# Key-value sums and quotients in two 64-column halves instead of four 32-column quarters, with a rewritten step list

## The chip, the cores and the metric

The kernel runs on one core of one Trainium2 chip. The metric is device time in microseconds of one execution; three executions of the kernel before gave 562.0 to 562.4 us, median 562.02 us. The trace that is read below is a fourth, profiled execution.

## What is computed

The input is q, k and v of 4 batches x 8 heads x 576 positions x 64. Attention with 128 random features comes first, then two layers of experts with one expert per token; the second layer reads what the first gives. In float32, cut to what matters here:

```python
q_p, k_p = phi(q_s), phi(k_s)                  # phi: project on omega (128 x 64), subtract a max, exp
kv = np.einsum('bhsm,bhsd->bhmd', k_p, v)      # sums of keys and values: 128 x 64 per head
z = np.sum(k_p, axis=2)
num = np.einsum('bhsm,bhmd->bhsd', q_p, kv)
den = np.einsum('bhsm,bhm->bhs', q_p, z)[..., None] + 1e-06
attn = num / den                               # the quotients
# x: 2304 tokens x 512; each of two layers, for each token's best of 8 experts e:
h = np.maximum(x[mask] @ w1[e], 0.0)           # 512 -> 1024
out[mask] = gate_w[mask, None] * (h @ w2[e])   # 1024 -> 512 (layer 1 has a second gate as well)
```

## The kernel before

**Attention.** Heads go in 16 pairs (0 to f). For a pair, TensorE projects keys (`k_proj`, L185) and queries (`q_proj`, L219) into tiles `ph`; VectorE takes maxima of the key features (L195), ScalarE makes their exponentials (L199); query features are copied out of PSUM by ScalarE or VectorE, GpSimd takes their maximum over partitions (L226), VectorE subtracts it (L230), ScalarE makes the exponential (L234). Then `kv` (L242) sums keys times values into `pkv`, a copy makes it `kvr`, `num` (L268) multiplies query features by it into `pn`, VectorE divides (L286 to L290), TensorE transposes (L304, `pf`), and copies give the raw activations.

**The two functions that change.** `kv` and `num` have a 128-partition output of 65 columns for each chunk of 128 positions and each head. They cut it into four matmuls, each with 32 columns of the stationary operand, that write to partitions 0, 32, 64 and 96. Each of these float32 matmuls is two matmuls and two weight loads in the trace: 640 in the program of each of `kv` and `num` are 1280 rows each.

**Experts.** Eight units (layer, batch) run in the order `ORDER`. A unit takes the expert that most of its batch chose, splits the expert's weights into a high and a low part (`high` L133 or L131, `low` L488), and multiplies in three terms (`group`, L92, `pm`): 384 matmuls of 288 columns in 64 steps of six. ScalarE and VectorE take each of the first 32 steps' results (`hh` L515, `hl` L516); VectorE multiplies each result of the last 32 by the gate (L534, `y`). `pm` has two PSUM buffers.

**The stray block.** Tokens that did not choose their batch's expert are handled in blocks of up to eight. The one block that these inputs need in layer two is done by `ahead` (flow `A`: choose it, load its data, find its tokens, gather them with GpSimd at L662, multiply by w1, L692 `pu`, transpose, L701 `phf`, multiply by w2, L713 `pyc`, transpose, L721 `pby`, scatter with GpSimd at L732 into `by`). It is then added to an earlier batch's output by `early` (flow `B`: load `old`, add at L753, store at L755) or to the last unit's own rows by `merge` (L548, steps `M7..`) before their store (L557, steps `S7..`). All of it is issued with factors that are zero where it does not apply, so both additions always run.

**What sets the order.** All engines' instructions are issued in the order of the string `PLAN`: a name is one step of attention (first letter the function, then the pair, then the part), of a unit (`F` fetch, `H` high, `L` low, `W` gate row, `X`, `Y` next layer's split, `S` store, `M` merge), of a flow (`G0` to `G7` gate of a unit, `A`, `B`); a `+` means VectorE in place of ScalarE; a number is so many steps of six matmuls of the running unit; `z5` is five idle matmuls on zeros (L836). Each engine runs its own instructions in this order, and waits on semaphores.

Of the kernel before, what the change touches and what calls it, by code (L numbers as in the profile page):

```python
# [48 lines left out]
r100 t01 m01 e010 e011 z5 q11 k10 k11 s00 m11 r110 v00 v01 x00 s01 w0 r111+ t10 m10 e111 e110 x01 z6 q20 k20 r200 s10
r201+ n00 n01 e100 m20 d00 e101 t11 s11 x10 d01 v10 v11 e200 k21 m21 e201 w1 x11 z5 f00 f01 q21 e210 g00 r211 e211  # L50
r210+ g01+ n10 n11 v20 v21 d10 t20 q30 q31 r301 s20 x20 r300+ r311 r310 h0 w2 o0 t21 d11 a5 a6 k30 m30 s21 t31 f10 g10
t30 l0 f11 k31 m31 e301 e300 g11 x21 q40 s31 r400 r401 q41 r410 r411+ a7 e310 h1 o1 e311 n20 n21 s30 d20 x31 d21 t40
l1 k40 k41 b6 x30 v30 v31 w3 f20 g20 m40 f21 s40 e400 m41 e401 g21 t41 s41 n30 n31 e411 e410 x40 d30 d31 h2 k50 k51
m51 x41 v40 v41 e510 f30 l2 e511 w4+ g30 m50 c6 f31 q50 r500 e500 r501+ n40 n41 q51 a8 r510 r511 d40 e501 d41 g31+ o2
b7 t50 t51 z6 k60 k61 h3 l3 m60 o3 m61 G0 v50 v51 G0 e601 e610 c7 s50 G0 G0 s51 f40 f41 g40 g41 G0 G0 x50 e600 w5 e611
o4 z3 k70 m70 x51 G0 P0 F00 F01 k71 m71 v60 v61 n50 e701 d50 e710 e700 c8 G0 w6 e711 n51 d51 q60 q61 H00 r610 a9 r600
r601+ v70 v71 f50 c9 f51 L00 G0 G0 w7+ H01+ t60 g50 g51 F02 1 L01 G0 1 o5 s60 1 F03 2 x60 2 H02+ W0 1 L02 2 H03 1 F04
1 L03 3 F05 1 H04+ 2 L04 2 H05+ 1 F06 1 L05 3 F07 1 H06+ 2 L06 9 H07 L07 2 r611+ t61 2 h4+ l4 h5+ 1 s61 b8 b9 1 l5 1
x61 1 n60 n61 q70 q71 r700 r710+ r711 d60 d61 r701+ aa 1 t70 2 f60 s70 t71 f61 k80 k81 x70 m80 m81 S010 ba g60+ g61+ 1
e801 e800 s71 1 e811 e810 1 h6+ o6 1 v80 v81 w8+ x71 n70 n71 q80 q81 ab r801 r811+ r810 d70 d71 r800+ l6 1 t81 2 f70  # L60
s81 f71 k90 ka0 m90 g70 g71 k91 e900 e901 bb m91 h7 x81 ma0 o7 t80 s80 1 G1 G1 l7 ea01 e910 1 G1 G1 x80 S020 1 G1 G1 1
G1 1 P1 F10 F11 2 G1 2 G1 G1 e911 ka1 G1 bc G2 v90 v91 H10 L10 G2 ma1 S030 w9 n80 n81 d80 d81 G2 W1 F12 G2 H11 1 ea11
ea10 1 L11 2 f80 g80 G2 G2 3 P2 G2 ea00 1 H12 1 G2 1 L12 2 G2 G2 F13 1 F14 G2 1 H13+ 2 L13 2 H14 1 F15 1 L14 3 F16 1
H15 2 L15 2 H16+ 1 F17 1 L16 2 f81 q90 q91 r910 r911+ g81 r901+ F20 r900+ ac S000 X00 Y00 1 t91 o8 h8+ H17+ 1 t90 1 l8
1 s91 L17 3 s90 1 H20 x91 X01+ Y01 1 X02+ F21 1 x90 L20 1 S100 1 Y02 X03+ ca cb 2 F22 1 Y03 1 H21 1 va0 va1 n90 n91 cc
wa qa0 qa1 ra00+ ra10 ra01 ad ra11+ L21 S110 d90 d91 1 ta0 ta1 1 F23 1 sa0 2 f90 f91 kb0 kb1 sa1 bd xa1 mb0 mb1 g90+
g91+ xa0 1 eb01 eb00 1 eb11 eb10 H22+ 1 h9+ na0 na1 vb0 vb1 da0 cd qb0 qb1 rb01+ rb10+ rb00 l9 rb11+ wb+ da1 ae L22 o9
S120 1 tb0 1 tb1 2 sb0 fa0 F24 ga0 2 sb1 xb0 1 xb1 H23 1 nb0 G3 nb1 db0 S130 L23 W2 qc0 qc1 F25 rc10 af rc01+ rc11
rc00 db1 G3 1 fb0 fb1 kc0 kc1 be mc1 gb0+ gb1 mc0 tc1 tc0 1 ec10 sc1 ec11 1 G3 G3 ob 1 ec01 ec00 sc0 1 xc1 1 G3 xc0 G3
1 H24 1 G3 P3 1 L24 3 F26 3 H25+ fa1 kd0 kd1 ga1+ md0 L25 bf md1 vc0 vc1 G4 oa ha+ F27 wc nc0 ed01 nc1 G4 G4 ed10 ce  # L70
dc0 dc1 la hb+ 2 fc0 gc0 1 lb 5 H26 2 L26 3 F30 3 X10 H27 Y10 3 L27 1 F31 4 H30 X11+ Y11 1 X12+ S200 1 L30 1 Y12 X13
Y13 2 F32 G3 ed00 3 H31+ G3 G3 G4 1 G3 L31 S210 1 G4 G4 2 G4 F33 1 P4 2 G4 1 H32 1 G4 L32 G4 1 S220 G4 1 F34 5 H33 1
S230 W3 1 L33 3 F35 3 H34+ 2 L34 3 F36 3 H35+ 2 L35 3 F37 3 H36+ 2 L36 3 F40 3 H37 2 L37 2 F41 4 H40+ 1 S300 1 L40 2
F42 4 H41 1 S310 1 L41 1 F43 5 H42+ 1 S320 1 L42 1 F44 5 H43+ 1 S330 1 L43 3 F45 3 H44 2 L44 3 F46 3 H45 fc1 qd0 qd1
rd00+ gc1 rd01 L45 rd11+ rd10 1 oc hc td0 1 F47 lc td1 2 sd0 2 ed11 1 xd0 sd1 1 H46 vd0 vd1 wd xd1 L46 cf ke0 kf0 kf1
me0 mf1 mf0 1 ef11 ef10 ee00 ee01 1 nd0 nd1 dd0 dd1 ef00 ef01 4 fd0 gd0 fd1 qe0 qe1 gd1 ke1 re00 re01+ hd+ me1 od re10
ld re11 te0 1 ee11 te1 1 H47 1 se0 1 L47 1 W4 1 se1 xe0 ee10 1 ve0 vf0 ve1 vf1 xe1 we+ ne0 ne1 qf0 rf00 rf01 de0 de1
wf+ 1 fe0 ge0 fe1 qf1 rf10 rf11+ ge1+ 1 he+ oe tf0 le tf1 2 sf0 1 X40+ 2 sf1 xf0 Y40 2 xf1 1 nf0 nf1 df0 df1 2 ff0 gf0
ff1 gf1+ 1 G5 G5 of hf 1 G5 G5 lf T 1 G5 G5 2 G5 1 P5 F50 F51 2 G5 S420 2 G5 G5 1 G5 1 H50+ 1 L50 2 F52 H51+ 1 S430 1
L51 3 F53 H52+ S410 1 L52 3 F54 1 H53+ 2 L53 2 H54+ 1 F55 1 L54 3 F56 1 H55 2 L55 2 H56 1 F57 1 L56 6 H57 S400 G6 1  # L80
L57 G6 G6 G6 2 G6 G6 W5 1 G6 1 P6 F60 F61 1 G6 2 G6 G6 X41 Y41 1 G6 S500 X50+ 2 Y50 1 H60+ 2 L60 2 H61 F62 X42 Y42 1
S510 X43 X51 1 L61 2 Y51 1 F63 3 H62 Y43 1 S520 X52+ 1 L62 Y52 2 F64 4 H63 1 X53+ Y53 S530 W6 1 L63 3 F65 3 H64+ 2 L64
# [869 lines left out]
```

## Time and profile before

| | |
|---|---|
| median of three runs | 562.02 us |
| profiled execution, its own time | 564.31 us |
| its span in the trace | 562.5 us |
| TensorE matmul busy | 532.2 us, 95% of the span, 6572 matmuls |
| TensorE weight loads | 506.6 us, 6572 loads |
| VectorE / ScalarE / GpSimd busy | 347.6 / 190.6 / 74.5 us |
| granted TensorE clock over the span | 0.985 of full speed |

The medians of runs and the span of the profiled execution differ by half a microsecond; the profiled execution's own time is 1.8 us over its span. Matmuls are pipelined, so that busy time on TensorE is not work at the engine's peak: what a group of matmuls costs is the time from its first start to the start of the next group.

### The profile page before, as it was taken

To read this page: it belongs to the slowest core of one execution; us is meant where nothing else is said; L and a number is where in the kernel's file an instruction comes from. 1 tells how busy PE (TensorE), PEld (TensorE's weight loads), DVE (VectorE), ACT (ScalarE), POOL (GpSimd) and SP (SyncE) were. 2 spreads that over 40 slices of the span, in tenths; PEclk is the share of its full clock that TensorE was granted. 3 is DMA by queue.
4 is the path that set the end of the run, shared out by engine and by line. 5 is a ranking of instruction groups with operands and counts; after the bars stand their busy time and mean duration, and the time that the engine had idled before them with its cause. 6 is when DMAs were issued, how large, how long until landed. Compare 5 with 4: busy or idle time off the path is not lost.

```text
span 562.5 us, 15495 instructions
## 1 busy us (share of the span) xinstructions
PE 532.2 (95%) x6572; PEld 506.6 (90%) x6572; DVE 347.6 (62%) x778; ACT 190.6 (34%) x484; POOL 74.5 (13%) x68
## 2 busy tenths in 40 slices
PE   6889999998999999999999999999999999999980
PEld 5667899887999998999999999899999999999970
DVE  3787875685677877575543467656666547445514
ACT  4687631343433345332220256221322231142000
POOL 4462101230021440000000022200000000000010
PEclk9999999998999999999999999999999999999996
DMA  8324742226355572324333333006444423435644
GB/s 321 117 87 147 247 138 81 86 87 178 97 170 192 147 225 81 101 100 145 90 113 118 118 97 68 24 23 212 129 126 155 121 72 97 155 97 152 238 160 174
DMA packets 83964, 74.34 MB, mean 132 GB/s; under 512 B 14256, under 2 KB 68144, under 8 KB 83888
## 3 DMA queue, kind: packets, MB, share of 16 engines
q1 hardware_dynamic: 83600, 73.15, 41.6%
q8 instruction: 53, 0.87, 0.6%
q14 instruction: 23, 0.19, 0.1%
q10 hardware_dynamic: 288, 0.13, 0.1%
HBM read 57.79 MB, written 15.48 MB: 130 GB/s over the span
## 4 chain that ended last, share of the span: by engine, by line
PE 91%; DVE 3%; ACT 3%; issue 2%; DMA 1%; POOL 0%; POOLq 0%; DVEq 0%; ACTq 0%
PE pm L92 73%; PE pn L268 4%; PE pkv L242 3%; PE ph L219 3%; PE ph L185 3%; PE pf L304 2%; PE pg L339 1%; ACT kp L199 1%; DMA om<-omst 1%; DVE old L753 1%; DVE y L548 1%; ACT qhh L133 0%; DVE qhh L230 0%; DVE nm L195 0%; PE idle L836 0%
## 5 line engine op out<-in xcount | busy, mean ns | idle before, releaser
L92 PE MATMUL pm<-xh,wh 128*128 128x288 f32 x512 | 152.7, 298 | 3.5 <-issue 2.5
L92 PE MATMUL pm<-hh,wh 128*128 128x288 f32 x512 | 153.7, 300 | 0.0
L92 PE MATMUL pm<-xh,wl 128*128 128x288 f32 x512 | 151.6, 296 | 0.0
L92 PE MATMUL pm<-xl,wh 128*128 128x288 f32 x512 | 151.3, 296 | 0.0
L92 PE MATMUL pm<-hh,wl 128*128 128x288 f32 x512 | 150.9, 295 | 0.0
L92 PE MATMUL pm<-hl,wh 128*128 128x288 f32 x512 | 150.8, 294 | 0.0
L516 DVE SCALAR_TENSOR_TENSOR hl<-pm,hh 128x288 fp32r<-128x288 f32 x128 | 58.5, 457 | 88.7 <-ACT hh L515 88.3
L226 POOL PARTITION_ALL_REDUCE qhl<-qhh x32 | 68.0, 2162 | 295.9 <-ACT qhh L133 153.6
L515 ACT ACTIVATE hh<-pm 128x288 fp32r<-128x288 f32 x128 | 52.8, 413 | 143.1 <-PE pm L92 143.0
L92 PEld LDWEIGHTS pm<-hh,wh 128*128 128x128 f32 x512 | 96.1, 188 | 4.6 <-issue 3.2
L92 PEld LDWEIGHTS pm<-xl,wh 128*128 128x128 f32 x512 | 96.6, 189 | 2.6 <-issue 2.6
L92 PEld LDWEIGHTS pm<-xh,wh 128*128 128x128 f32 x512 | 96.7, 189 | 2.5 <-DVE hl L516 1.6
L92 PEld LDWEIGHTS pm<-xh,wl 128*128 128x128 f32 x512 | 96.6, 189 | 0.0
L92 PEld LDWEIGHTS pm<-hl,wh 128*128 128x128 f32 x512 | 96.1, 188 | 0.0
L92 PEld LDWEIGHTS pm<-hh,wl 128*128 128x128 f32 x512 | 96.0, 188 | 0.0
L488 DVE TENSOR_TENSOR wl<-wr,wh 128x1024 fp32r<-128x1024 f32 (+1 forms) x72 | 78.6, 1099 | 5.4 <-ACT wh L133 5.2
L534 DVE TENSOR_TENSOR y<-pm,cb 128x288 f32<-128x288 f32 x64 | 29.1, 455 | 58.4 <-PE pm L92 58.2
L133 ACT CAST wh<-wr 128x1024 fp32r<-128x1024 f32 (+1 forms) x40 | 38.2, 960 | 63.2 <-PE pm L92 57.8
L199 ACT ACTIVATE kp<-ph,nm 128x128 f32<-128x128 f32 x140 | 40.2, 393 | 6.8 <-DVE nm L195 6.7
L195 DVE TENSOR_REDUCE nm<-ph 128x3 f32<-128x384 f32 (+1 forms) x64 | 27.7, 482 | 7.4 <-PE ph L185 7.2
L230 DVE TENSOR_TENSOR qhh<-qhh,qhl 128x576 f32<-128x576 f32 x32 | 30.8, 961 | 1.6 <-POOL qhl L226 1.6
L234 ACT ACTIVATE qhh<-qhh 128x576 f32<-128x576 f32 x32 | 22.3, 712 | 26.1 <-DVE qhh L230 26.1
(128 smaller groups left out, 443.9 us busy)
## 6 DMA issues: line engine op xcount, KB each, us to landing
wr<-w2a SPq DMA_DIRECT2D x16, 512.0 KB, 3.6
wr<-w2b SPq DMA_DIRECT2D x16, 512.0 KB, 3.6
wr<-w1a SPq DMA_DIRECT2D x12, 512.0 KB, 4.3
wr<-w1b SPq DMA_DIRECT2D x12, 512.0 KB, 3.8
vt<-vp SPq DMA_DIRECT2D x16, 325.0 KB, 5.0
qr<-qT SPq DMA_DIRECT2D x16, 288.0 KB, 3.6
kr<-kT SPq DMA_DIRECT2D x16, 288.0 KB, 3.8
xd<-xraw SPq DMA_DIRECT2D x16, 288.0 KB, 3.4
```

The costliest lines, as they stand in the source:

```text
L92: nc.tensor.matmul(out, ws(*t), xs(*t), start=first and t == terms[0], stop=last and t == terms[-1])
L133: nc.scalar.copy(out=out, in_=in_)
L195: nc.vector.tensor_reduce(out=nm[:, j, 0:m], in_=pk, axis=AX.X, op=ALU.max, negate=True)
L199: nc.scalar.activation(self.kp[:, c, j * NF : (j + 1) * NF], self.pk[part][j][:, i * NF : (i + 1) * NF], AF.Exp, bias=self.nm[part][:, j, ...
L226: nc.gpsimd.partition_all_reduce(qm, qe, 128, bass_isa.ReduceOp.max)
L230: nc.vector.tensor_tensor(out=qe, in0=qe, in1=qm, op=ALU.subtract)
L234: nc.scalar.activation(qe, qe, AF.Exp)
L268: nc.tensor.matmul(ps[32 * g : 32 * g + 32, x, w], self.q[j][0][:, c0 + 32 * g : c0 + 32 * g + 32], self.kvr[:, w], start=True, stop=True,)
L488: nc.vector.tensor_tensor(out=wl[:, p], in0=self.raw[i][:, p], in1=wh[:, p].bitcast(F32), op=ALU.subtract)
L515: nc.scalar.activation(hh[:, s], pm, AF.Relu)
L516: nc.vector.scalar_tensor_tensor(out=hl[:, s], in0=pm, scalar=0.0, in1=hh[:, s].bitcast(F32), op0=ALU.max, op1=ALU.subtract)
L534: nc.vector.tensor_tensor(out=y[:, t], in0=pm, in1=self.cb[:, t], op=ALU.mult)
```

## The change

`kv` and `num` cut their output into two matmuls of 64 stationary columns (partitions 0 and 64) in place of four of 32, so that the program has 320 of them in each in place of 640. The moved operand, 65 columns, is the same in each.

`PLAN` is another list. It has the same steps apart from idle matmuls: 11 (`z8`, `z3`) in place of 25. The steps of attention, fetches and splits stand elsewhere, and which of the copies VectorE does differs (20 of 64 query copies in place of 26). The stray block's flows come earlier: of the 512 steps of six matmuls, before, `A` has its last pieces and `B` all of its pieces behind the 512th; now `A` ends behind the 480th, `B` behind the 481st, and of the last unit's stores and merges only `M731` and `S710` to `S731` stand behind the 512th.

```diff
-a0 I b0 a1 b1 b2 c0 c1 c2 b3 b4 b5 a2 a3 a4 c3 c4 c5 J q00 k00 q01 r000 m00 r001+ r010 r011 e000 e001 t00 k01 q10 r101
...
-H75 2 L75 F77 3 H76+ 2 L76 6 H77 2 L77 1 G7 W7 1 A A A A A A 4 A 2 A 3 A 1 A A A A A A 13 A 5 A A A A A A A A A A A
-A B B B B M710 B M700 M720 M730 M731 S710 B B S700 S720 S730 S731 B B B B B
...
+F74 3 A 1 S630 W7 H73 2 L73 F75 A A A A A A 6 H74+ 2 L74 F76 6 H75 2 L75 F77 3 A A A 1 A A 2 H76 2 L76 4 A A 1 A A 1 A
+A A A H77+ B B B B B B B B B B B 1 B 1 L77 7 M700 S700 8 M710 8 M720 4 M730 3 S710 S720 S730 M731 S731
...
-                for g in range(4):
+                for g in range(0, NF, 64):
                     nc.tensor.matmul(
-                        self.pkv[32 * g : 32 * g + 32, w],
-                        self.kp[:, c, j * NF + 32 * g : j * NF + 32 * g + 32],
+                        self.pkv[g : g + 64, w],
+                        self.kp[:, c, j * NF + g : j * NF + g + 64],
                         self.vt[:, c, w],
...
-                    for g in range(4):
+                    for g in (0, 64):
                         nc.tensor.matmul(
-                            ps[32 * g : 32 * g + 32, x, w],
-                            self.q[j][0][:, c0 + 32 * g : c0 + 32 * g + 32],
+                            ps[g : g + 64, x, w],
+                            self.q[j][0][:, c0 + g : c0 + g + 64],
                             self.kvr[:, w],
```

TensorE early in the program, before the first unit, from the first pair's transposes on: `ph` are projections, `pkv` and `pn` the two functions that change. Before:

```order
L219 MATMUL ph<-qr,om 128x288 x2
L268 MATMUL pn<-kvr,qhh 32x65 x40
L242 MATMUL pkv<-vt,kp 32x65 x40
L219 MATMUL ph<-qr,om 128x288 x4
L185 MATMUL ph<-om,kr 128x128 x6
L304 MATMUL pf<-ident,xt 128x128 x4
L304 MATMUL pf<-ident,xt 128x64
L185 MATMUL ph<-om,kr 128x128 x4
L219 MATMUL ph<-qr,om 128x288 x4
L268 MATMUL pn<-kvr,qhh 32x65 x40
```

And with the change (a line number is one less there):

```order
L218 MATMUL ph<-qr,om 128x288 x2
L267 MATMUL pn<-kvr,qhh 64x65 x20
L241 MATMUL pkv<-vt,kp 64x65 x20
L218 MATMUL ph<-qr,om 128x288 x2
L184 MATMUL ph<-om,kr 128x128 x10
L218 MATMUL ph<-qr,om 128x288 x2
L267 MATMUL pn<-kvr,qhh 64x65 x20
L218 MATMUL ph<-qr,om 128x288 x2
L303 MATMUL pf<-ident,xt 128x128 x4
L303 MATMUL pf<-ident,xt 128x64
```

A pair's sums and quotients have half as many matmuls, and the projections between two pairs' quotients stand in another order; per pair there are as many projections and transposes as before.

VectorE at the end of the program, from the last of the block's search (`at`) in the kernel before. Before:

```order
L653 TENSOR_SCALAR at<-top_7514 1x8
L534 TENSOR_TENSOR y<-pm,cb 128x288 x5
L724 TENSOR_TENSOR yw<-pby,xg 128x128
L548 SCALAR_TENSOR_TENSOR y<-by,state,y 128x576
L753 SCALAR_TENSOR_TENSOR old<-by,state,old 128x576
L548 SCALAR_TENSOR_TENSOR y<-by,state,y 128x576 x2
L548 SCALAR_TENSOR_TENSOR y<-by,state,y 128x288 x2
L753 SCALAR_TENSOR_TENSOR old<-by,state,old 128x576 x3
```

And with the change, from the block's last product on:

```order
L723 TENSOR_TENSOR yw<-pby,xg 128x128
L515 SCALAR_TENSOR_TENSOR hl<-pm,hh 128x288
L130 CAST wh<-wr 128x1024
L752 SCALAR_TENSOR_TENSOR old<-by,state,old 128x576 x4
L487 TENSOR_TENSOR wl<-wr,wh 128x1024
L533 TENSOR_TENSOR y<-pm,cb 128x288 x2
L547 SCALAR_TENSOR_TENSOR y<-by,state,y 128x576
L533 TENSOR_TENSOR y<-pm,cb 128x288 x2
```

The block's scaled product `yw` and the four additions to `old` now stand ahead of all eight of the last unit's gate products (L533), and the merges stand between these. On TensorE, `pu` has six matmuls of the unit behind it, then come `phf`, 48 matmuls, `pyc`, six matmuls, `pby`, and 198 matmuls to the end.

## Rows read from the trace of the kernel before

**Rows 1.** Busy time by stage: PE, PEld, DVE, ACT, POOL (instructions), clock, DMA share, GB/s.

```profile
4.44:63.86 59.42, 54.20 (x1427) 43.05 (x1428) 45.35 (x119) 42.58 (x135) 25.36 (x13) 0.97 0.53 173
63.86:544.20 480.34, 475.47 (x5082) 461.75 (x5081) 295.20 (x648) 146.06 (x346) 46.38 (x31) 1.00 0.41 125
544.20:562.50 18.30, 2.51 (x68) 1.82 (x65) 6.80 (x11) 0.65 (x2) 1.53 (x8) 0.71 0.52 187
```

**Rows 2.** The page: the chain of work that ended last.

```profile
PE 91%; DVE 3%; ACT 3%; issue 2%; DMA 1%; POOL 0%; POOLq 0%; DVEq 0%; ACTq 0%
```

**Rows 3.** End of the program: timelines of PE, then of DVE and of SP.

```profile
544.91 1.95 PE L713 MATMUL pyc<-w,h 128*32 128x128 f32 x64 [0.47 <-ACT h L703]
547.25 0.33 PE L721 MATMUL pby<-ident,yc 128*128 128x128 f32 x1 [0.39 <-ACT yc L715]
...
544.25 0.46 DVE L534 TENSOR_TENSOR y<-pm,cb 128x288 f32<-128x288 f32 x1 [2.74 <-PE pm L92]
550.11 0.82 DVE L548 SCALAR_TENSOR_TENSOR y<-by,state,y 128x576 f32<-128x576 f32 x1 [2.13 <-POOL by L732]
...
555.46 1.52 SPq L755 DMA_DIRECT2D outT<-old  x3
```

**Rows 4.** Waits of PE over the whole span: time in total, times, longest.

```profile
PE pn L268 <- issue: 2.8, 3, 1.6
PE pm L92 <- issue: 2.5, 1, 2.5
PE pkv L242 <- issue: 2.3, 2, 1.3
PE pm L92 <- DVE hl L516: 1.0, 1, 1.0
```

**Rows 5.** PE's timeline at one of these gaps.

```profile
16.25 1.01 PE L268 MATMUL pn<-kvr,qhh 128*32 128x65 f32 x56
18.88 0.55 PE L268 MATMUL pn<-kvr,qhh 128*32 128x65 f32 x24 [1.62 <-issue]
```

**Rows 6.** Windows from one gap to the next (columns as in rows 1).

```profile
18.00:25.50 7.50, 6.12 (x253) 5.15 (x253) 4.38 (x12) 4.64 (x15) 1.85 (x1) 1.00 0.12 44
25.50:37.80 12.30, 10.78 (x252) 7.95 (x251) 11.54 (x24) 8.68 (x25) 10.68 (x6) 1.00 0.41 121
```

**Rows 7.** The page: one of the DMA queues, packets, MB, share.

```profile
q8 instruction: 53, 0.87, 0.6%
```

**Rows 8.** Windows behind two of the gaps: PE busy, granted clock, DMA.

```profile
40.00:44.00 4.00, 4.00 (x103) 0.58 0.01 4
136.00:140.00 4.00, 3.93 (x20) 0.63 0.46 149
```

**Rows 9.** PE's timeline at a key projection, then at sums and quotients.

```profile
105.28 1.44 PE L185 MATMUL ph<-om,kr 64*128 64x128 f32 x20
106.65 0.40 PE L92 MATMUL pm<-hh,wh 128*128 128x288 f32 x1
...
110.01 1.34 PE L242 MATMUL pkv<-vt,kp 128*32 128x65 f32 x80
111.17 1.08 PE L268 MATMUL pn<-kvr,qhh 128*32 128x65 f32 x59
...
120.41 1.19 PE L339 MATMUL pg<-xraw,wg 128*32 128x144 f32 x32 [0.18 <-ACT kp L199]
```

**Rows 10.** Groups by line and shape, PEld: weight loads.

```profile
L185 PEld LDWEIGHTS ph<-om,kr 64*128 64x128 f32 x320 | 23.8, 203 | 3.3 <-ACT qhh L133 0.8 <-issue 0.6 <-ACT kp L199 0.5
L268 PEld LDWEIGHTS pn<-kvr,qhh 128*32 128x32 f32 x1280 | 20.5, 113 | 6.3 <-issue 3.8 <-ACT xraw L133 1.1 <-ACT kp L199 0.8
```

**Rows 11.** The chain that ended last, in order of time, before the first unit.

```profile
13.96 0.76 PE idle L836 x6
...
27.46 0.40 ACT qhh L133
...
58.40 0.86 ACT kp L199 x3
```

More of the change, by code (lines that the diff above doesn't have):

```diff
@@ L47 @@
 PLAN = """
-a0 I b0 a1 b1 b2 c0 c1 c2 b3 b4 b5 a2 a3 a4 c3 c4 c5 J q00 k00 q01 r000 m00 r001+ r010 r011 e000 e001 t00 k01 q10 r101
[L49 to L82, printed above, removed]
@@ L83 @@
-3 F66 3 H65 2 L65 3 F67 3 H66+ 2 L66 6 H67 G7 1 L67 G7 G7 G7 2 G7 G7 1 G7 1 P7 F70 F71 1 A G7 1 A 2 G7 G7 1 A 1 A S600
-1 H70+ A 2 L70 2 A H71 2 F72 L71 1 S610 2 F73 3 H72+ 1 S620 1 L72 1 F74 5 H73 1 S630 1 L73 3 F75 3 H74 2 L74 3 F76 3
-H75 2 L75 3 F77 3 H76+ 2 L76 6 H77 2 L77 1 G7 W7 1 A A A A A A 4 A 2 A 3 A 1 A A A A A A 13 A 5 A A A A A A A A A A A
-A B B B B M710 B M700 M720 M730 M731 S710 B B S700 S720 S730 S731 B B B B B
+a0 I a1 b0 b1 c0 c1 c2 J a2 a3 a4 b2 b3 b4 b5 c3 c4 c5 q00 q01 k00 r001 r010+ k01 r000 t00 r011+ m00 t01 q10 r101+
@@ new lines @@
+e000 e001 m01 r100+ s00 z8 q11 e010 e011 r111 r110 k10 x00 m10 k11 s01 t11 m11 v00 v01 e100 q20 x01 w0+ r201+ e101
+r200 e110 s11 e111 t10 n00 n01 q21 k20 a5 r211 r210 d00 d01 s10 x11 m20 v10 v11 x10 t20 f00 w1 e201 g00+ f01 k21 g01+
+o0 m21 h0+ e200 s20 t21 q30 e211 e210 r301 r300 n10 n11 v20 v21 q31 x20 a6 s21 d10 k30 d11 w2 m30 r311 t31 l0 r310 x21
+k31 q40 r400 r401+ e300 e301 t30 m31 n20 n21 e311 q41 e310 a7 d20 s31 r411 f10 g10 s30 f11 k40 x31 g11+ o1 m40 t41
+r410 x30 d21 v30 v31 s41 h1 l1 e401 e400 k41 m41 b6 t40 w3 f20 g20 x41 f21 k50 g21 o2 m50 s40 e411 e410 n30 n31 v40
@@ new lines @@
+v41 c6 e500 h2+ e501 l2 w4 q50 q51 a8 x40 r500 r501 d30 r510 d31 r511 n40 n41 f30 d40 d41 g30 f31 k51 g31 b7 m51 o3 h3
+t50 s50 t51 G0 e510 G0 e511 l3 k60 k61 G0 v50 v51 m60 e601 w5 G0 x50 b8 c7 e600 s51 x51 m61 G0 G0 z3 k70 e610 e611 G0
+m70 P0 F00 F01 k71 m71 n50 v60 v61 e700 n51 c8 e710 e711 G0 w6 e701 d50 d51 f40 f41 G0 G0 G0 g40 g41 o4 v70 v71 f50
+f51 H00+ L00 F02 g50 g51+ o5 W0 q60 q61 a9 H01 r600+ r611 r610+ 1 L01 F03 1 t60 2 s60 1 H02 1 x60 1 L02 F04 6 H03 1
+L03 F05 2 H04 2 L04 F06 5 H05+ 1 L05 F07 3 H06+ c9 1 L06 3 w7 2 H07 1 L07 6 S000 1 r601+ 1 t61 2 s61 2 q70 q71 r711 aa
@@ new lines @@
+x61 r710 r701+ r700 1 t71 1 S010 n60 n61 s71 t70 d60 d61 1 x71 1 s70 1 h4+ 1 x70 l4 f60 f61 n70 n71 d70 d71 g60+ g61+
+o6 h5 l5 2 f70 g70 f71 q80 q81 r801 ab g71+ G1 G1 o7 r800 r810 h6+ l6 h7+ l7 r811 1 G1 t80 G1 1 t81 S020 G1 G1 2 s80
+G1 2 x80 P1 F10 F11 1 s81 1 G1 2 q90 q91 ac r911+ r910 S030 G1 G1 G2 H10+ G2 L10 F12 r900 k80 k81 H11 m81 t90 G2 1
+e811 e810 L11 F13 1 s90 2 x90 2 H12 2 H13 L12 F14 2 L13 F15 7 H14+ 1 L14 F16 1 H15 2 L15 F17 6 H16 1 L16 4 H17 X00+
+Y00 2 L17 1 m80 G1 W1 2 e800 e801 3 v80 v81 ca w8 X10 S100 X01 Y01 1 Y10 X02+ 3 Y02 X03 Y03 2 G2 1 r901+ 1 G2 G2 S110
@@ new lines @@
+t91 1 X11+ 1 G2 1 Y11 P2 F20 F21 s91 b9 1 G2 1 x91 2 x81 1 G2 n80 n81 X12 H20 Y12 d80 S120 G2 d81 1 L20 F22 1 H21+ 1
+f80 f81 k90 k91 m90 L21 F23 m91 g80 g81+ o8 1 e900 e901 2 e911 e910 ba bb 2 S130 H22 1 L22 F24 X13+ 2 H23+ Y13 1 L23
+F25 qa0 qa1 ka0 ra00 ad ra10 ka1 bc ta0 ma1 ma0 ra11+ ra01 1 ea11 ea10 1 sa0 ea00 ea01 1 ta1 1 H24 xa0 v90 v91 va0 va1
+cb cc L24 wa F26 sa1 w9 kb0 kb1 kc0 mc0 xa1 mb1 bd mb0 1 ec01 ec00 1 eb10 eb11 1 eb01 eb00 G3 G3 n90 n91 na0 na1 vb0
+vb1 d90 da0 da1 d91 cd qb0 qb1 ae rb10+ rb11+ rb00 rb01 wb 1 f90 f91 kd0 kd1 g90 g91 kc1 mc1 be tb0 sb0 o9 tb1 md1 bf
@@ new lines @@
+md0 1 ec11 1 xb0 sb1 fa0 ga0+ ed10 ed11 1 ed00 ed01 1 H25+ 2 fa1 qc0 qc1 af L25 F27 rc11 rc00+ ga1+ oa rc10 rc01 2 tc1
+1 tc0 1 sc1 2 H26+ 1 xc1 sc0 ec10 1 L26 6 h8 H27+ 2 L27 l8 h9 l9 ha 1 la G2 W2 5 S200 8 S210 1 G3 G3 1 G3 G3 2 P3 F30
+F31 G3 xb1 2 G3 1 nb0 nb1 G3 G3 G3 qd0 qd1 rd11 db0 db1 rd01+ rd10 rd00 1 fb0 S220 gb0+ H30 td1 fb1 1 H31 L30 F32 1
+L31 F33 sd1 3 xd1 gb1+ ob 1 hb lb 2 H32 W3 S230 G4 G4 L32 F34 1 H33+ G4 G4 L33 F35 1 G4 G4 3 G4 1 P4 2 G4 vc0 vc1 vd0
+vd1 G4 H34 ke0 L34 F36 ce me0 G4 ke1 me1 G4 wc+ cf wd+ 1 ee01 1 ee10 ee11 6 H35+ 2 L35 F37 6 H36 2 L36 F40 6 H37+ 2
@@ new lines @@
+L37 F41 6 H40 S300 2 L40 F42 6 S310 H41+ 2 L41 F43 6 S320 H42+ 2 L42 F44 6 W4 S330 H43+ 2 L43 F45 6 H44 2 L44 F46 6
+H45+ 2 L45 F47 6 H46 2 L46 6 H47 2 L47 1 xc0 nc0 nc1 dc0 dc1 1 td0 sd0 1 fc0 fc1 qe0 gc0 qe1 gc1+ xd0 hc+ lc re00 re01
+nd0 nd1 re10+ te0 re11+ dd0 oc dd1 ee00 ve0 ve1 we te1 1 se0 2 fd0 xe0 fd1 kf0 kf1 mf0 gd0+ gd1 S400 od se1 mf1 X40 1
+ef00 hd+ ef01 1 qf0 qf1 rf10 rf11 rf00+ ef10 ld ef11 rf01 xe1 1 tf0 2 vf0 ne0 ne1 vf1 sf0 de0 de1 xf0 wf tf1 sf1 2 fe0
+xf1 ge0+ fe1 ge1 oe nf0 nf1 df0 df1 he le 1 S410 1 ff0 gf0 ff1 gf1 of 1 hf+ lf G5 G5 T 1 G5 G5 1 G5 G5 2 G5 1 P5 F50
@@ new lines @@
+F51 1 S420 G5 3 G5 G5 G5 2 H50+ 1 L50 F52 1 H51 2 L51 F53 4 H52+ 1 L52 F54 2 H53+ 2 L53 F55 5 H54 1 L54 F56 3 H55+ 1
+L55 F57 5 H56+ 1 L56 6 H57 Y40 G6 1 X41 G6 L57 Y41 X42 1 Y42 G6 G6 X43+ 1 W5 1 Y43 G6 G6 3 G6 1 P6 S500 F60 F61 G6 8
+H60+ S510 2 H61+ L60 F62 1 L61 F63 5 S520 S430 2 H62 2 L62 F64 4 S530 H63 2 L63 G7 G7 F65 1 G7 5 H64+ 2 L64 F66 6 H65
+G6 G7 G6 G6 1 W6 L65 F67 1 G7 G7 2 G7 1 P7 1 A 1 G7 1 A H66 2 G7 G7 G7 L66 F70 1 A 3 A 2 A H67+ X50 Y50 1 X51 1 Y51
+X52+ 2 A 1 L67 F71 2 Y52 X53+ 1 H70 S600 1 A A A A A A 1 L70 F72 1 Y53 5 S610 H71 2 L71 F73 6 S620 1 A 2 H72+ A 1 L72
```

## The prediction

> **What bounds the kernel now.** I read the chain that ended last first: 91% of it is TensorE [rows 2]. Then the busy time by stage [rows 1]. From 63.86 to 544.20 us, where units run, TensorE is busy for 475.5 of 480.3 us: there the sum of its work is the time, and the other engines matter only where they make it wait. Before 63.86 us, with attention alone, it is busy for 54.2 of 59.4 us, VectorE for 45.4 and ScalarE for 42.6; the chain of that stage changes over to ScalarE and VectorE in five places, from 0.4 to 7.8 us long, of which the second begins and the last is what the rows show [rows 11], for 14.9 us in all. Behind 544.20 us there are 18.3 us with hardly any TensorE work: the stray block's second product, its transpose, the scatter on GpSimd, additions and stores, one behind the other [rows 3]. So three things can be had: the tail, TensorE's waits, and its work.
>
> **TensorE's waits.** The largest are put down to no engine: "issue", 2.8 + 2.5 + 2.3 = 7.6 us in six gaps [rows 4], five of them inside sums and quotients, like the one where 56 of 80 matmuls run, then nothing for 1.62 us, then the other 24 [rows 5]. Between three such gaps TensorE ran 253 + 253 and 252 + 251 matmuls and loads [rows 6]: about twice 250. The program has 6572 + 6572 of them, and the instruction queue moved 53 packets [rows 7]: 248 for each packet. So I take these gaps as TensorE out of instructions: blocks of some 250 run out faster than the next arrives. A pair's sums are 80 matmuls and 80 loads in 1.16 us, 110.01 to 111.17 [rows 9]; at that rate 250 instructions last 1.8 us. The Trainium skill, "Runtime: NRT & Kernel Launch", section "Instruction fetch mechanics", has blocks of 16 KiB or 256 instructions too, but says that crossing into the next is mostly hidden. The trace agrees on the size, and differs on the hiding by the 7.6 us; by the page alone the gaps would stay (rival three).
>
> **The change, part by part.**
>
> *Fewer instructions.* Sums and quotients go from 2560 matmuls and 2560 loads to half, so a run of them uses 250 instructions in some 3.6 us at the least, if its time stays the same. What a block takes to arrive I bound by the gaps: the run's 1.8 us plus 1.0 to 2.5 us, so 2.8 to 4.3 us. The gaps should go, or shrink to some tenths. Each costs a little more than its idle time, since the last matmul's draining is hidden otherwise: the 24 behind the gap take 0.55 us and not 24/80 of 1.16, so 0.2 us [rows 5, 9]; 7.6 + 6 x 0.2 = 8.8 us. Behind two gaps, of 1.3 and 2.5 us without a matmul, the granted clock is 0.58 and 0.63 over 4 us, since half (1.2 of 2.4 GHz) is granted for part of it [rows 8]: 4 x (0.42 + 0.37) = 3.2 us of work lost. Of these, 1.0 + 2.5 us of idle time, 0.4 us of draining and 1.5 us of clock are at 136 and 356 us, where TensorE bounds; with the smallest gap **-5.6 us**. If only half of the gaps went it would be -2.8.
>
> *The stage before the first unit.* Three of the gaps (1.6, 1.0, 1.3 us, with draining 4.5 us), the other 1.7 us of clock, and 14 idle matmuls less are there; six take 0.76 us [rows 11], so 1.8 us. That is 8.0 us of TensorE time. VectorE's 45.4 us and ScalarE's 42.6 us stay, and part of the 14.9 us on their chain will take the place of what goes; the list is another one, so its sign is open. I take **-5.5 us**, from -1 (they take all of it back) to -11 (they overlap better too; VectorE's 45.4 us are the floor).
>
> *Time of a half.* Not in the trace: 64 stationary columns. Four quarters move 65 columns each side by side: 80 in 1.16 us, so 58 ns for a round of four; a gate's 32 matmuls with the same loads and 144 columns take 1.19 us, 149 ns a round [rows 9]. So a round's time follows the moved columns, not the number of matmuls, and those stay: 58 ns for a round of two. The nearest row with wider loads is the key projection, 64 x 128 loads, 128 columns moved, two side by side: 20 in 1.37 us [rows 9], 137 ns a round for twice the columns, 68 for 65. Bounds: 640 rounds x 0 to 10 ns, 0 to +6.4 us; since a load of 64 is between the two, and most of the projection's excess is at its start, I take **+1.5 us**. Faster than 58 ns the moved columns exclude.
>
> *Block amid the last unit.* The last `pm` ends at 544.2 us. What follows it is then its gate product (0.46 us), half a merge (0.82 us for 576 columns, so 0.4), and the last store; before, the last store is issued at 556.98 us and the span ends 5.5 us later [rows 3]. So 0.5 + 0.4 + 0.4 + 5.5 = 6.8 us in place of 18.3: **-11.5 us**. `pyc` (1.95 us) and the two transposes move into TensorE's stream, with a return to `pm` behind each: **+2.4 us**. What hides the rest: between `pyc` and `pby` six matmuls, 0.8 us, must cover the copy of 0.27 us; behind `pby`, VectorE waits some 2 us for the scatter and adds four times 0.8 us ahead of the unit's gate products, some 7 us after `pby`, while two PSUM buffers give TensorE 0.8 + 2 x 3.2 = 7.2 us. That is just covered. If it is late, `pm` waits for VectorE.
>
> *New waits among the units.* The old list leaves TensorE 1.0 us on VectorE there [rows 4]. The new one has attention packed into fewer places, and a few blocks' second weights are due 54 matmuls (7.2 us) after the first product: **+2 us**, from 0 to 8.
>
> Sum: -5.6 - 5.5 + 1.5 - 11.5 + 2.4 + 2 = -16.7 us. Against the profiled execution's 564.31 us that is 547.6 us; the median of the runs shown is 2.3 us under that execution, so the median should be 562.0 - 16.7 = **545.3 us**.
>
> **Rivals.**
>
> 1. *Weight loads come out of hiding; slower.* The loads of a quarter take 113 ns in the records and those of 128 columns 203 [rows 10], 0.94 ns a column, so a load of 64 streams for 60 ns, as long as the moved columns. If a half's loads can't run under the matmuls in flight, a round takes 58 + 60 = 118 ns: 640 x 60 = +38 us in place of the 1.5, and 562 - 18 + 38 = 582 us. Against it: the projection's 128-column loads are hidden under 128 columns moved. For it: they go to two halves of the rows, and here all 128 rows are used. It decides once a round costs 18.2/640 us = 28 ns more. The Trainium skill, "TensorE: Matmul & The Clock Gate", section "Part 3: Packing small matmuls — row/col tiling", says that loads overlap with matmuls in flight only where their row groups differ, and by that a half's would not. The quarters in the trace have the same row groups and 58 ns a round, just what their moved columns need, so the trace does not agree with it as it stands.
> 2. *ScalarE and VectorE bound the first stage.* Then -1 there: 549.8 us. For it speak the 14.9 us; against it that the chain is on TensorE, not on them, on both sides of each gap in that stage.
> 3. *The gaps are not a matter of the number of instructions* and stay, with their clock: 5.6 us among units and all but 1.8 of 5.5 us before them come back, 545.3 + 5.6 + 3.7 = 555 us. Against it: the even counts between gaps.
> 4. *The block holds up the last unit*: a second product that waits for its weights, or VectorE behind the scatter, 3 to 8 us of `pm` waiting: 548 to 553 us.
>
> **How the numbers follow.** The forecast 0.62 (540 to 549 us), rival two 0.15, rival four 0.10, rival three 0.06, rival one 0.07. The range reaches from the forecast's bounds (first stage at -11, no cost of halves, no new waits: 536) to 555 us, which takes in rivals two to four and leaves out rival one and what lies beyond. All but rival one are faster; 0.2%, 1.1 us, is about what a measurement can tell from no change. Faster 0.92, same 0.02, slower 0.06.
>
> **What would show it.** Waits on "issue" near zero in TensorE's list, and the instruction queue with some ten packets less (2588 instructions / 248). Sums of a pair in 40 matmuls and 1.16 to 1.3 us. The span's end some 7 us behind the last `pm`. No stretch of low clock at 40 and 136 us. The first unit's first `pm` at about 58 us. Wrong if a pair's sums take over 1.7 us, if "issue" keeps more than 4 us, or if `pm` waits on VectorE for more than 5 us.

## The result, and the profile after

| us | before | after |
|---|---|---|
| median (runs) | 562.21 (4) | 542.08 (4) |
| lowest to highest | 562.0 to 564.37 | 541.7 to 543.32 |
| profiled execution, own time | 564.31 | 542.09 |
| its span | 562.5 | 540.3 |

The ratio is 0.9637, with an interval from 0.9609 to 0.9666: faster. The forecast was 545.3 us, with a range from 536 to 555.

Read by stage first, as [rows 1] were. Busy time after, in the same columns:

```profile
4.16:54.63 50.47, 48.85 (x854) 39.96 (x854) 44.60 (x122) 40.51 (x132) 24.50 (x12) 1.00 0.62 207
54.63:534.10 479.47, 478.54 (x4427) 463.20 (x4425) 295.66 (x648) 150.49 (x358) 48.12 (x39) 1.00 0.43 131
534.10:540.30 6.20, 0.00 (x1) 0.00 (x0) 0.98 (x2) 0.00 (x0) 0.00 (x0) 0.78 0.09 30
```

The first stage went from 59.4 to 50.5 us, the units from 480.3 to 479.5, the tail from 18.3 to 6.2: -8.9, -0.9 and -12.1 us; TensorE's first instruction is 0.3 us earlier as well. The first and the second stage stand at full clock throughout. In the units' stage TensorE now idles for 0.9 us of 479.5, where it idled for 4.9.

Then TensorE's waits, which answer to [rows 4]; the first one listed, 4.2 us, is the wait for the first data at the program's start:

```profile
PE ph L218 <- DVE om L816: 4.2, 1, 4.2
PE pn L267 <- ACT kp L198: 0.4, 1, 0.4
PE pm L91 <- DVE y L533: 0.3, 1, 0.3
PE pn L267 <- ACT qhh L132: 0.3, 1, 0.3
PE pm L91 <- DVE hl L515: 0.3, 1, 0.3
```

"issue", 7.6 us before, has gone from the list, and no wait on an engine took its place; `pm`'s wait for `hl` went from 1.0 to 0.3 us. The instruction queue, in the page's list of queues, moved ten packets less than in [rows 7]:

```profile
q8 instruction: 43, 0.70, 0.6%
```

TensorE's timeline in the first stage and at a pair's sums among the units shows 40 matmuls in a run where [rows 9] had 80. From the start of a run to the start of what follows it takes 1.22, 1.27 and 1.32 us:

```profile
20.37 1.39 PE L267 MATMUL pn<-kvr,qhh 128*64 128x65 f32 x40
21.59 1.34 PE L241 MATMUL pkv<-vt,kp 128*64 128x65 f32 x40
22.86 0.76 PE L218 MATMUL ph<-qr,om 64*128 64x288 f32 x4
...
94.96 1.39 PE L267 MATMUL pn<-kvr,qhh 128*64 128x65 f32 x40
96.28 0.40 PE L91 MATMUL pm<-hh,wh 128*128 128x288 f32 x1
```

At the end, VectorE's timeline, to be laid beside [rows 3]: the block's product and its additions to `old` stand among the last unit's work, and behind the last `pm` there is one gate product and one merge, then 5.15 us of a store:

```profile
507.37 0.29 DVE L723 TENSOR_TENSOR yw<-pby,xg 128x128 f32<-128x128 f32 x1 [2.16 <-PE pby L720]
...
510.19 3.01 DVE L752 SCALAR_TENSOR_TENSOR old<-by,state,old 128x576 f32<-128x576 f32 x4 [0.59 <-POOL by L731]
513.11 1.22 DVE L487 TENSOR_TENSOR wl<-wr,wh 128x1024 fp32r<-128x1024 f32 x1
514.25 0.82 DVE L533 TENSOR_TENSOR y<-pm,cb 128x288 f32<-128x288 f32 x2
...
534.14 0.46 DVE L533 TENSOR_TENSOR y<-pm,cb 128x288 f32<-128x288 f32 x1 [2.18 <-PE pm L91]
534.63 0.52 DVE L547 SCALAR_TENSOR_TENSOR y<-by,state,y 128x288 f32<-128x288 f32 x1
```

VectorE's first gate products, at 514.25, come just late enough for `pm` to wait 0.3 us.

### The profile page after: what moved, and what is told of

The parts are those of the page before. It is cut to its first block, busy times and chain, and to the rows that moved or that the text cites. A ratio compares the mean times of both kernels' runs of the same rounds, so it can differ in the third digit from the quotient of the medians.

```text
span 540.3 us, 12897 instructions
## 1 busy us (share of the span) xinstructions
PE 527.4 (98%) x5278; PEld 503.2 (93%) x5278; DVE 341.5 (63%) x772; ACT 192.3 (36%) x490; POOL 73.9 (14%) x68
## 4 chain that ended last, share of the span: by engine, by line
PE 87%; DVE 8%; DMA 2%; ACT 1%; issue 1%; POOL 1%; POOLq 0%; DVEq 0%
PE pm L91 72%; PE ph L218 3%; PE pn L267 3%; PE ph L184 3%; PE pkv L241 2%; DVE nm L194 2%; PE pg L338 1%; DVE qhh L229 1%; PE pf L303 1%; DMA wr<-w1a 1%; DVE xt L289 1%; DMA om<-omst 1%; DVE wl L487 1%; ACT kp L198 0%; DVE old L752 0%
## 5 line engine op out<-in xcount | busy, mean ns | idle before, releaser
L225 POOL PARTITION_ALL_REDUCE qhl<-qhh x32 | 65.9, 2099 | 284.0 <-DVE qhh L130 99.7
L533 DVE TENSOR_TENSOR y<-pm,cb 128x288 f32<-128x288 f32 x64 | 29.0, 455 | 69.6 <-PE pm L91 64.2
L132 ACT CAST wh<-wr 128x1024 fp32r<-128x1024 f32 (+1 forms) x39 | 36.9, 961 | 52.2 <-PE pm L91 32.6
L229 DVE TENSOR_TENSOR qhh<-qhh,qhl 128x576 f32<-128x576 f32 x32 | 28.9, 905 | 1.0 <-POOL qhl L225 0.9
```

What stands on the lines that cost most here:

```text
L132: nc.scalar.copy(out=out, in_=in_)
L225: nc.gpsimd.partition_all_reduce(qm, qe, 128, bass_isa.ReduceOp.max)
L229: nc.vector.tensor_tensor(out=qe, in0=qe, in1=qm, op=ALU.subtract)
L533: nc.vector.tensor_tensor(out=y[:, t], in0=pm, in1=self.cb[:, t], op=ALU.mult)
```

## The experiments

Theory: TensorE ran out of instructions in blocks of some 250, and half as many instructions for sums and quotients end that; the tail is worth its length; the wider loads cost little. Against it stood the four rivals of the prediction. Each kernel was profiled once, and the table reads its trace as above. "Pairs" is the time of all sums and quotients, their gaps included; "low clock" lists where a stretch at half clock begins ahead of the tail, and how long it is.

| kernel | span | first stage | units | tail | packets | pairs | low clock |
|---|---|---|---|---|---|---|---|
| before | 562.5 | 59.4 | 480.3 | 18.3 | 53 | 47.4 | 40.0 and 135.6 (3.4 each) |
| after | 540.3 | 50.5 | 479.5 | 6.2 | 43 | 41.1 | none |
| halves_alone | 556.5 | 54.9 | 478.7 | 18.4 | 43 | 41.7 | none |
| list_alone | 553.0 | 58.0 | 483.9 | 6.3 | 53 | 50.9 | none |
| end_alone | 553.8 | 59.5 | 483.5 | 6.3 | 53 | 48.1 | none |
| all_but_end | 549.6 | 50.1 | 476.3 | 18.4 | 43 | 41.1 | none |
| whole | 575.2 | 68.5 | 496.3 | 6.1 | 38 | 76.5 | 59.1 (13.7) |
| num_quarters | 546.1 | 52.2 | 483.0 | 6.1 | 48 | 44.3 | none |
| no_idle | 541.0 | 50.8 | 479.3 | 6.1 | 43 | | none |
| again | 541.4 | 51.0 | 479.5 | 6.4 | 43 | | none |
| idle_25 | 540.9 | 51.2 | 478.8 | 6.3 | 43 | | none |
| split_first | 541.6 | 50.9 | 480.1 | 6.2 | 43 | | none |
| halves_no_idle | 557.2 | 54.9 | 479.1 | 18.5 | 43 | | none |
| shift24 | 567.8 | 66.1 | 482.2 | 18.4 | 54 | 52.5 | 63.1 and 175.8 (3.4 each) |

`again` is the changed kernel once more: its span is 1.1 us longer than in the first trace, its first stage 0.5 us. Smaller differences between two traces are not read here. The first stage of `shift24` begins with 24 idle matmuls that were put ahead of it.

### The code without the list, and the list without the code

`halves_alone` has the list of before, and only this edit; `list_alone` has the new list and the reverse of it.

```diff
-                for g in range(4):
+                for g in range(0, NF, 64):
...
-                        self.pkv[32 * g : 32 * g + 32, w],
-                        self.kp[:, c, j * NF + 32 * g : j * NF + 32 * g + 32],
+                        self.pkv[g : g + 64, w],
+                        self.kp[:, c, j * NF + g : j * NF + g + 64],
...
-                    for g in range(4):
+                    for g in (0, 64):
...
-                            ps[32 * g : 32 * g + 32, x, w],
-                            self.q[j][0][:, c0 + 32 * g : c0 + 32 * g + 32],
+                            ps[g : g + 64, x, w],
+                            self.q[j][0][:, c0 + g : c0 + g + 64],
```

> The two functions in halves, with the list of steps of before. If TensorE ran out of instructions because quarters use them up too fast, waits on 'issue' fall from 7.6 us to under 1 us and the two stretches of low clock go; of the 8.8 + 3.2 us some 3 us go back to ScalarE and VectorE before the first unit, and the wider loads cost some 2 us: about 555 us. If the gaps belong to the old list and not to the number of instructions, they stay, and the wider loads alone are seen: 563 to 565 us.

> The new list with quarters. If the number of instructions makes the gaps, they come back, elsewhere in the program but at the same count of instructions within a block (six or more of 1 to 2.5 us, some with low clock behind them): 542 + 8 to 12 - 2 = 548 to 552 us, and the instruction queue has 53 packets again. If the list had removed them, no gap, and 540 to 541 us, since quarters save the wider loads.

Against the kernel before, `halves_alone` is at 0.9861 (0.9804 to 0.9919), `list_alone` at 0.9801 (0.9739 to 0.9863). TensorE's waits of `halves_alone`:

```profile
PE pm L92 <- DVE hl L516: 2.2, 3, 1.0
PE pkv L242 <- DMA vt<-vp: 1.1, 1, 1.1
PE ph L185 <- DVE qhh L131: 0.5, 1, 0.5
```

and of `list_alone`, with two windows of its busy time that reach from one gap to the next (columns as in [rows 1]):

```profile
PE pkv L241 <- issue: 6.8, 6, 1.5
...
PE pn L267 <- issue: 2.0, 1, 2.0
```

```profile
194.50:204.30 9.80, 8.39 (x253) 7.84 (x253) 5.54 (x15) 5.72 (x21) 0.00 (x0) 1.00 0.47 147
204.30:268.80 64.50, 63.29 (x763) 59.93 (x763) 42.99 (x109) 23.38 (x60) 12.53 (x6) 1.00 0.43 124
```

With the code alone every "issue" gap is gone; with the list alone there are seven, 8.8 us, and no stretch of low clock follows any of them, where the expectation had it behind some. They stand in other steps than before, but again a whole number of blocks apart: 253 + 253 = 506, and 763 + 763 = 1526, 3.02 times as many, though the second stretch takes 6.6 times as long. Rival three falls. The code brings -6.0 us of span with the old list, and -12.7 with the new one (553.0 to 540.3): the two edits give 22.2 together, 15.5 one by one. This is read from single traces: the ratios of the runs, 1.4 and 2.0% less one by one and 3.6% together, each known to 0.3 to 0.6%, do not by themselves show that the two edits help each other. With the old list part of the gain went into waits that the gaps had covered, for data of `vt` and for `hl`.

### The end of the list alone, and all but the end

Cut at the 353rd step of six matmuls of the units, where the old list's end is replaced by the new one's (with quarters), and the reverse (with halves). The rows of VectorE's order ahead of the prediction show this piece of the list.

```diff
 # end_alone: PLAN, the last lines
-... H77 2 L77 1 G7 W7 1 A A A A A A 4 A 2 A 3 A 1 A A A A A A 13 A 5 A ... A B B B B M710 B M700 ...
+... 1 A A A A H77+ B B B B B B B B B B B 1 B 1 L77 7 M700 S700 8 M710 8 M720 4 M730 3 S710 ...
```

> The list of before up to the 353rd step of the units and the new one from there on, with quarters: the block amid the last unit and nothing else of the change. If the tail's gain is kept, 18.3 us behind the last matmul of the units become 6.2 us and TensorE gets some 2.5 us more work: 552 to 553 us. If the block's pieces make the units' matmuls wait as much as they save, 558 to 562 us.

> The change up to the 353rd step, the list of before from there on: halves and the new order of attention, with the block behind the last unit. If the parts add up, 542.1 + 9.5 = 551 to 552 us, and with the run of the end alone the two gains make up the 20 us of the whole. If the parts help each other (the end gains less without the rest, or more), the sum of the two is off by over 2 us.

Ratios 0.9824 (0.9763 to 0.9885) and 0.9744 (0.9688 to 0.98). The end brings -8.7 us, all but the end -12.9: -21.6 of the -22.2 together, so in the traces these two add; by the ratios it is 4.3% against 3.6%, the same within their intervals. With either code the end takes 12.0 or 12.2 us off the tail and puts 3.2 us onto the units (480.3 to 483.5, 476.3 to 479.5).

`end_alone` also keeps the gaps, and no stretch of low clock follows them. Its windows around the two that had one before (PE busy, granted clock, DMA), and the gaps inside them, 1.06 and 1.69 us here, 1.30 and 2.52 before:

```profile
37.00:44.00 7.00, 5.68 (x213) 1.00 0.17 47
134.00:140.00 6.00, 4.31 (x35) 1.00 0.61 157
```

```profile
38.58 0.30 PE L242 MATMUL pkv<-vt,kp 128*32 128x65 f32 x2 [1.06 <-issue]
...
135.85 0.29 PE L92 MATMUL pm<-xh,wh 128*128 128x288 f32 x1 [1.69 <-issue]
```

Its first stage is 59.5 us nonetheless, where before, with 3.4 us at half clock, it was 59.4.

### Whole width, and quarters for the quotients

In the changed kernel, one matmul of 128 columns for both (`whole`), and quarters for `num` alone (`num_quarters`):

```diff
 # whole
-                for g in range(0, NF, 64):
+                for g in range(0, NF, NF):
...
-                    for g in (0, 64):
+                    for g in (0,):
 # num_quarters
-                    for g in (0, 64):
+                    for g in (0, 32, 64, 96):
```

> The new list, with all 128 stationary columns in one matmul in place of two halves: a quarter of the instructions of before. If the loads run beside the matmuls, but one after another once they cannot be split over column groups, a 128-column load of some 110 ns bounds each matmul, where 65 moved columns take 58: 20 matmuls of a pair's sums take 2.2 us in place of 1.3, 32 such runs cost 25 to 32 us more, 567 to 575 us. If loads are no bound, 1.2 us and 540 to 542 us. If a load cannot start before the matmul ahead of it is through, 3.3 us a run and 600 us or more.

> The new list, sums in halves and quotients in quarters: half of the instructions that the change saved are back. If what counts is how long a block of some 250 instructions lasts, only blocks that fall mostly on quotients run out: two to five gaps on 'issue', 2 to 5 us in total, 545 to 549 us. If the gaps came with the whole of the quarters' 10 blocks alike, half of the list alone's gain lost: 548 us; if sums alone made them, none and 541 us.

`whole` is slower than the kernel before, at 1.0158 (1.0111 to 1.0206); `num_quarters` is at 0.9673 (0.9641 to 0.9705). TensorE's timeline of `whole` at a pair's sums:

```profile
171.03 2.34 PE L241 MATMUL pkv<-vt,kp 128*128 128x65 f32 x20
173.17 0.38 PE L91 MATMUL pm<-hh,wh 128*128 128x288 f32 x1
```

20 matmuls take 2.14 us, 107 ns each. At the 0.94 ns a column that the prediction took from [rows 10], 128 columns of weights load in 120 ns: a matmul takes no longer than its load, so the 65 moved columns are all hidden, although each load goes to the same rows as the matmul in flight. The Trainium skill, "TensorE: Matmul & The Clock Gate", section "Part 3: Packing small matmuls — row/col tiling", lets loads overlap only where row groups differ, in its list of what overlaps, and by that the two would add. This run does not agree with that; it agrees with a sentence ahead of it in the same section, by which a load may also go ahead of matmuls in flight into the background weight buffer. So the width decides: 32 and 64 columns load within the time of the moved columns, 128 don't. Over 32 runs a pair's sums or quotients, from start to next start, take 1.28 us (median) in quarters, 1.32 in halves, and 2.28 whole (2.15 at the least). The step from halves to whole is 32 x 0.96 = 30.7 us. With what the half clock from 59.1 us on adds to those that lie in it, the column "pairs" grows by 35.4 us, which is all of the 34.9 us between the spans.

`num_quarters` has gaps again, in two places, and five packets more:

```profile
PE pn L267 <- issue: 1.5, 1, 1.5
...
PE pkv L241 <- issue: 0.7, 1, 0.7
```

Quarters for one of the two functions thus bring back 2.2 us of "issue", for both (`list_alone`) 8.8.

### More instructions ahead of the first gap

In the kernel before, 24 idle matmuls at the start of the list, 24 matmuls and 24 loads:

```diff
-a0 I b0 a1 b1 b2 c0 c1 c2
+a0 I z24 b0 a1 b1 b2 c0 c1 c2
```

> The kernel before with 24 idle matmuls more (24 matmuls and 24 loads) ahead of the first projection, in time in which TensorE waits for its first data. If a gap stands at the end of a block of 256 instructions, each gap moves up by 48 instructions, that is 24 matmuls: the first from behind 56 of the first pair's 80 quotient matmuls to behind 32. If it is a wait for another engine or for data, it stays behind 56. The time is within 3 us of before either way.

TensorE's timeline of `shift24` at the first two gaps:

```profile
15.93 0.67 PE L268 MATMUL pn<-kvr,qhh 128*32 128x65 f32 x32
18.00 0.89 PE L268 MATMUL pn<-kvr,qhh 128*32 128x65 f32 x48 [1.41 <-issue]
18.68 1.34 PE L242 MATMUL pkv<-vt,pxh 128*32 128x65 f32 x80
21.61 0.60 PE L185 MATMUL ph<-om,kr 64*128 64x128 f32 x5 [1.58 <-issue]
```

Before, the gap stood behind 56 of the same 80 matmuls [rows 5]; now it stands behind 32. It moved by just the 24 matmuls that were put ahead of it, so its place is set by the number of instructions that TensorE has run, not by a tile. The next two old gaps move in the same way, from behind 47 and 78 of 80 matmuls of a pair's sums to behind 23 and 54. Before, then in `shift24`:

```profile
26.03 0.67 PE L242 MATMUL pkv<-vt,kp 128*32 128x65 f32 x33 [1.04 <-issue]
38.34 0.30 PE L242 MATMUL pkv<-vt,kp 128*32 128x65 f32 x2 [1.30 <-issue]
...
26.75 1.01 PE L242 MATMUL pkv<-vt,kp 128*32 128x65 f32 x57 [0.88 <-issue]
39.29 0.64 PE L242 MATMUL pkv<-vt,kp 128*32 128x65 f32 x26 [1.54 <-issue]
```

The two long gaps at 136.07 and 357.37 us keep their counts as well, at 137.07 and 362.29 in `shift24`: in both traces TensorE runs 1646 matmuls and 1647 loads from the last gap shown to the one, and 2548 and 2547 from there to the other.

In `shift24` a further gap, the second in its timeline above, comes 48 + 80 matmuls behind the first, 256 instructions with their loads, ahead of a projection where before there was none: a block's end falls there now.

The traces also hold the times of the instruction queue's packets, of 16 KiB each. In the five kernels that have gaps on "issue", all 28 of these gaps end 1.0 to 1.6 us after such a packet has landed: before, packets land at 17.52, 24.58 and 36.95 us, and TensorE goes on at 18.88, 26.03 and 38.34. So a gap is a wait for a block of instructions, seen from both sides. In the changed kernel, counted at 254 records of TensorE to a packet, every packet lands 2.7 us or more ahead of its block's first matmul (an estimate, for the count is not exact).

The expectation on the time failed: one run took 569.64 us beside a median of 564.38 for before, 5.3 us more and not within 3. The idle matmuls are not what it went to, since the first pair's quotients start at 15.93 us, 0.3 earlier than before [rows 5]. TensorE waits 9.4 us on "issue" in place of 7.6, and 2.0 us for `y`, for which it did not wait before; the rest is open.

### The idle matmuls

The new list has 11 idle matmuls, the old one 25. `no_idle` is the changed kernel without any, `idle_25` has 25 again, `halves_no_idle` is `halves_alone` without its 25.

```diff
 # no_idle: m01 r100+ s00 z8 q11   and   G0 G0 z3 k70
-z8
-z3
 # idle_25
-z8
+z22
```

> The change without its 11 idle matmuls. If they only take TensorE's time before the first unit, 0.5 to 1.3 us less; if ScalarE and VectorE bound that stage, no change; if they keep the clock up, a stretch of low clock and 1 to 3 us more.

> The changed kernel once more, on the chip of the next three, so that they can be compared with it: the same ratio to the kernel before as at first, 0.961 to 0.967.

> The change with 14 idle matmuls more at the place of its first eight, 25 as before. If TensorE bounds that place, 1.5 to 1.8 us more; if ScalarE and VectorE do, under 0.5 us more.

> Halves with the list of before, without any of its 25 idle matmuls. If these are what the old list loses to the new one before the first unit, the stage falls from 54.9 us to 52 us or less and the time by 2 to 3 us against halves with the full old list. If the order of the other steps is what counts, the stage stays within 1 us of 54.9 us.

Ratios to before: `no_idle` 0.9618 (0.9595 to 0.9641), `again` 0.9625 (0.9599 to 0.9651), `idle_25` 0.9625 (0.9594 to 0.9656), `halves_no_idle` 0.9899 (0.9866 to 0.9932), all with the spans and first stages of the kernels they are variants of, within 0.8 us. Idle matmuls, 0 to 25 of them, cost and bring nothing in this kernel: where they stand, TensorE has time to spare.

### The last split ahead of the additions

The wait of 0.3 us of `pm` for `y` might be had by moving the last low part (`L77`, 1.22 us on VectorE) ahead of the block's additions to `old`:

```diff
-A A A A H77+ B B B B B B B B B B B 1 B 1 L77 7 M700
+A A A A H77+ L77 B B B B B B B B B B B 1 B 1 7 M700
```

> The change with the last weight split's second half (step L77) ahead of the block's additions, so that VectorE does it in the 2 us in which it waits for the scatter. VectorE is then 1.1 us earlier at the unit's first gate product, and the wait of 0.3 us of the units' matmuls on it goes: 0.3 to 0.6 us less, about what can be measured; no change if something else holds TensorE there.

0.962 (0.9595 to 0.9644), beside 0.9625 for `again`: the same. VectorE's timeline, with the one row of GpSimd's that it waits for:

```profile
512.66 3.00 DVE L752 SCALAR_TENSOR_TENSOR old<-by,state,old 128x576 f32<-128x576 f32 x4 [0.34 <-POOL by L731]
515.59 0.81 DVE L533 TENSOR_TENSOR y<-pm,cb 128x288 f32<-128x288 f32 x2
```

```profile
509.19 3.44 POOL L731 COPY by<-yw 128x4 f32 x8 [19.75 <-DVE yw L723]
```

The split filled VectorE's wait for the scatter, but the scatter took 3.44 us here and 2.34 in the changed kernel, so the additions began 3.91 us behind the start of the block's product `yw` in place of 2.82, which used up what the split had freed, and the wait stayed at 0.3 us. Why the scatter was slower is open: GpSimd ran while VectorE was busy instead of waiting, which is a reason only argued.

No kernel here is faster than the changed one by more than the noise.

## Why the prediction held, and where its terms were off

**Instruction gaps among the units (-5.6): right in cause.** Three runs show it: the gaps go with the code alone, stay with the list alone a whole number of blocks apart, and move by just as many matmuls as are put ahead. The packets that land just ahead of each gap's end say the same. The Trainium skill's page that the prediction named beside them, "Runtime: NRT & Kernel Launch", section "Instruction fetch mechanics", has the crossing into the next block mostly hidden; in halves the trace agrees, in quarters the kernel before has gaps of 0.2 to 2.5 us.

**The clock (1.5 us of it there, 1.7 in the first stage): its price is not shown.** No low clock is left after the change, as forecast. But a gap does not bring it by its length: 1.30 us was followed by it before, while 1.62 in the same trace [rows 5], 1.59 in `end_alone` and 2.02 in `list_alone` were not; in `shift24` one stretch follows a wait of 1.98 us for `y`. The first stage of `end_alone` is as long without low clock as that of before with it, so there it was worth no more than the half microsecond by which two traces differ. Over the 29 runs of the kernel before that were made beside the experiments, though, those with the lower mean clock (0.984 to 0.991) are the longer ones, by some 0.6 us for each thousandth, and a stretch of 3.4 us at half clock is 3 thousandths of the span. No run changes the clock alone, so a longer gap and the low clock behind it can't be told apart in this.

**Wider loads (+1.5): right.** 32 runs x 0.04 us = +1.3. (The upper bound there was a little low: 137 ns for 128 columns are 70 ns for 65, not 68, so 640 x 12 ns, +7.4 us.) Rival one falls at 64 columns, since loads do run under the matmuls in flight. One width further, `whole` is slower than before, because the load itself is then the longest part.

**Tail (-11.5): -12.1.** 0.46 of gate product, 0.52 of merge and 5.15 of store make the 6.2 us left. The forecast's 6.8 has 0.4 us twice, where its text names one half merge; that is most of the difference.

**The block in TensorE's stream (+2.4): +3.2** by two pairs of kernels. Of this `pyc`, the transposes and the returns behind them are the 2.4, the wait on `y` is 0.3, and the rest I can't assign. Rival four, 3 to 8 us of waiting, did not come: the cover, reckoned as just enough, fell short by 0.3 us.

**New waits (+2): too high.** `pm` now waits 0.3 us for `y`, and 0.7 less for `hl`. `all_but_end`, which has no block in the stream, is at -4.0 among the units. The gaps' -5.6 and the loads there (18 of the 32 runs, +0.7) leave +0.9 for everything else; without the 1.5 of clock in the 5.6 they leave -0.6. So what the clock was worth among the units can't be told from these either.

**First stage (-5.5): the mis-sized term, -8.9.** It was made of 4.5 us of gaps, 1.7 of clock and 1.8 of idle matmuls, 8.0 in all, of which VectorE and ScalarE were to take 2.5 back. `halves_alone` gives -4.5: the gaps came out whole, with the loads' price. The clock gave nothing that can be seen, nor did the idle matmuls. In their place the order of the new list gives -4.4 more (54.9 to 50.5), and only with halves: with quarters it gives -1.4 (59.4 to 58.0), for there four gaps, 2.02 + 1.28 + 0.38 + 1.47 = 5.2 us, fall into the stage, and three before, 4.0 us. At 0.2 us of draining each, the four are 6.0 of the 7.5 us between `list_alone` and the changed kernel in this stage. The prediction had said that the new order's sign was open, and put no number on it. What the order does is read from the chain that ended last, in time:

```profile
24.32 1.02 DVE nm L194 x2
...
31.28 1.55 DVE qhh L229
32.83 0.67 DVE xl L321
...
41.37 0.95 DVE qhh L229
42.99 0.93 DVE nm L194 x2
...
51.30 0.56 DVE xt L289
53.78 0.69 DVE wl L487
```

From 24.3 us to the first unit it runs mostly over VectorE (with 3.7 us of ScalarE and 0.9 of TensorE), which is busy for 44.6 of the stage's 50.5 us: the floor that the prediction named (45.4) is now near. So rival two's mechanism came, but at -8.9 and not at -1. TensorE's records fill still more of the stage, 48.9 us, but 14 idle matmuls more (`idle_25`), 1.8 us of work, lengthened it by only 0.2 us beside `again`. That VectorE bounds the stage is read from the chain; no run took work from it. The list also changes which engine makes a copy: VectorE and ScalarE are busy for 44.8 and 42.1 us of the stage in `halves_alone`, and for 44.6 and 40.5 with the new list. No run takes that apart from the order.

Together, by stage: first stage -8.9 for -5.5, units -0.9 for +0.3 with the loads, tail -12.1 for -11.5. That is 5.2 us beyond the sum in the traces; by the medians, 562.21 to 542.08, it is 20.1 us in place of 16.7, since the profiled execution of before was 2 us above its median and that of after was not.
